# A gated feed-forward and a linear attention in one kernel: order written by hand against order left to the framework's scheduler

## The chip, the cores and the metric

The kernel runs on one core of one Trainium2 chip. The metric is the device time of one execution in microseconds; where several executions are shown, their median counts.

A core has five engines, each with its own instruction queue that is worked off in order: TensorE (PE in the profile, matrix products; PEld is its weight loads), VectorE (DVE), ScalarE (ACT), GpSimd (POOL) and SyncE (SP, which here only issues DMAs). They wait for one another on semaphores. An instruction that waits holds up everything behind it on its engine, whether that is ready or not. So for each engine the order of its instructions is part of the program, and it is this order that the two kernels differ in.

## The reference

Two branches read the same layer-normalised input of 2048 tokens by 512 channels; their sum and the input itself are the output.

```python
xn = layernorm(x)
return x + A(xn, wqkv, w_phi, wo) + B(xn, w_gate, w_up, w_down)

def A(x, wqkv, w_phi, wo):                    # 32 heads of 16 channels
    q, k, v = heads(x @ wqkv)
    pq, pk = q @ w_phi, k @ w_phi             # per head
    phi_q = concat(softmax(pq), softmax(-pq)) # likewise phi_k from pk
    kv = phi_k.T @ v                          # summed over all tokens
    z  = sum over tokens of phi_k
    o  = (phi_q @ kv) / (phi_q @ z + 1e-6)
    return o @ wo

def B(x, w_gate, w_up, w_down):               # 1792 hidden channels
    return ((x @ w_gate) * (x @ w_up)) @ w_down
```

Matrix data are bf16, sums are f32. Branch A needs `kv` over all tokens before any token's output can start; branch B (called the GLU below) needs only its own tokens.

## The kernel before

Tokens are handled in 16 tiles `n` of 128, and in 4 groups `T` of 512. All names and lines of this section are those of the kernel before.

**Inputs and head.** Every load is issued from SP, in the order written (lines 86 to 99): two single tiles of x, the small `w_phi`, the key part of `wqkv` transposed by the DMA (`wkT`), the value part `wv`, then x and the GLU weights in growing pieces. Ten matrix products on zeros (`warm`, L130) run while the first x is on its way. `LNs`, `LNr` and `LNx` normalise one tile: statistics on DVE (L198, L200), the reciprocal root by two ACT instructions (L204, L205), the scaling on DVE (L209). The channel-major copy `xnT` that the products need is made by PE for tiles 0 to 3 (`TRpe`), and for groups 1 to 3 by a store to DRAM and a transposing DMA back (`TRst`). `foldj` multiplies `w_phi` into the key weights (`W1k`) and later into the query weights (`W1q`), one 128-row block at a time.

**Key pass, one step per tile** (loop at L323). `PK` makes the products for the keys, `EX` takes both exponentials on ACT, `RED`, `RCP` and `PHI` (L273, L279, L284) sum, invert and scale them on DVE, `VV` makes the values, and `KV` adds eight small products into three PSUM banks that stay open over all tiles. In each step the program puts three GLU units `G` at chosen places. A unit is one 128-channel block `f` of the hidden layer for one token group: four products with `wg` (L143), a copy to SBUF on ACT (L146), four products with `wu` (L149) and the elementwise product on DVE (L151) into `hT`. The PSUM results come from one pool of three buffers (`ps_gu`, tag `gu`), shared with the output stage.

**Query pass, one step per tile** (loop at L414). The sums are masked into `KVZ` (L364, L367). `Pq` makes the query products and exponentials of a quarter group. `ND` makes numerators and denominators with eight small products into one four-bank PSUM tile (`nd`, one buffer), and a chain on DVE finishes them: `rsm` (L393), `rho` (L395), `tmp` (L397), `sm` (L400), `rden` (L402). The next `ND` may start when `sm` has read the tile. POOL makes the output tokens `o_tok` (L404), which go to DRAM and come back transposed, once per group, into the place of `xnT`. `Fin` makes a tile's output: 14 products with `wd` (L161) and 4 with `wo` (L164) into a `gu` buffer, the residual sum on DVE (L166), the store. From the sixth step on, each step runs one `Fin` beside one `ND`, and the last `Fin` is cut into two column halves.

**What sets the order.** `ctx.enter_context(tc.manual_schedule())` (L63) keeps every engine's instructions in the order in which the program writes them; the calls in the two loops are that order. Memory places and semaphores are still set by the framework.

Of the kernel before, what the change touches and what calls it, by code (L numbers as in the profile page):

```python
# [8 lines left out]
BF16 = mybir.dt.bfloat16  # L9
# [12 lines left out]
def kernel(  # L22
# [35 lines left out]
    wT_pool = ctx.enter_context(tc.tile_pool(name="wT", bufs=1))  # L58
    hpool = ctx.enter_context(tc.tile_pool(name="hpool", bufs=1))
    gpool = ctx.enter_context(tc.tile_pool(name="gpool", bufs=3))  # L60
    opool = ctx.enter_context(tc.tile_pool(name="opool", bufs=3))
    ps_gu = ctx.enter_context(tc.tile_pool(name="ps_gu", bufs=3, space=PSUM))
    ctx.enter_context(tc.manual_schedule())  # L63
# [8 lines left out]
    xnT = xpool.tile([P, DC, S], BF16, name="xnT")  # L72
    oT = xnT
    W1k = wpool.tile([P, DC, D], BF16, name="W1k")
    W1q = wpool.tile([P, DC, D], BF16, name="W1q")
    KVZ = wpool.tile([P, 2, CQ, HC, J], BF16, name="KVZ")
    hT = [hpool.tile([P, FC, TT], BF16, name=f"hT{T}") for T in range(NT // GT)]
# [4 lines left out]
    def dma_cols(w, src, slo, lo, hi, eng):  # L82
        eng.dma_start(out=w[:, :, lo:hi], in_=src[:, slo + lo:slo + hi].rearrange("(c p) f -> p c f", p=P))

    wkT = wT_pool.tile([P, DC, D], BF16, name="wT")
    dma_x(0, 1)
    dma_x(1, 2)
    nc.sync.dma_start(out=wphi[:], in_=A_w_phi.rearrange("(c h) d f -> (h d) c f", c=DC))
    nc.sync.dma_start_transpose(out=wkT[:], in_=A_wqkv[:, D:2 * D])  # L89
    dma_cols(wv, A_wqkv, 2 * D, 0, D, nc.sync)  # L90
    dma_x(2, 4)
    for lo, hi in ((0, 256), (256, 768)):
        dma_cols(wg, B_w_gate, 0, lo, hi, nc.sync)
        dma_cols(wu, B_w_up, 0, lo, hi, nc.sync)
    dma_x(4, 8)
    dma_cols(wg, B_w_gate, 0, 768, F, nc.sync)
    dma_cols(wu, B_w_up, 0, 768, F, nc.sync)
# [6 lines left out]
    warm = consts.tile([P, TT], BF16, name="warm")  # L104
    nc.vector.memset(warm[:], 0.0)
    ident = consts.tile([P, P], BF16, name="ident")
    make_identity(nc, ident[:])

    BO16 = consts.tile([P, HC, DH], BF16, name="BO16")
    nc.gpsimd.memset(BO16[:], 1.0)  # L110
    nc.gpsimd.affine_select(out=BO16[:], in_=BO16[:], pattern=[[-DH, HC], [0, DH]],
                            compare_op=ALU.is_ge, fill=0.0, base=0, channel_multiplier=1)
    nc.gpsimd.affine_select(out=BO16[:], in_=BO16[:], pattern=[[DH, HC], [0, DH]],
                            compare_op=ALU.is_ge, fill=0.0, base=DH - 1, channel_multiplier=-1)
    NVT = 4
# [3 lines left out]
    BD = wT_pool.tile([P, DC, HC, DH], BF16, name="BD")  # L119
    for c in range(DC):  # L120
        nc.gpsimd.tensor_tensor(out=BD[:, c], in0=BO16[:],
                                in1=_bcast_ap(wphi[:, c, :], [wphi.ap[0], [0, HC], [1, DH]]), op=ALU.mult)
# [5 lines left out]
    wps = ps_gu.tile([P, TT], F32, name="gu")  # L128
    for i in range(10):
        nc.tensor.matmul(wps[:], lhsT=warm[:, 0:P], rhs=warm[:], start=True, stop=True)  # L130

    glu_done = [0]

    def G(k=1):
        for _ in range(k):
            i = glu_done[0]
            if i >= FC * (NT // GT):
                return
            glu_done[0] += 1
            T, f = divmod(i, FC)  # L140
            gps = ps_gu.tile([P, TT], F32, name="gu")
            for c in range(DC):
                nc.tensor.matmul(gps[:], lhsT=wg[:, c, f * P:(f + 1) * P], rhs=xnT[:, c, T * TT:(T + 1) * TT],  # L143
                                 start=(c == 0), stop=(c == DC - 1))
            g_sb = gpool.tile([P, TT], BF16, name="g_sb")
            nc.scalar.copy(out=g_sb[:], in_=gps[:])  # L146
            ups = ps_gu.tile([P, TT], F32, name="gu")
            for c in range(DC):
                nc.tensor.matmul(ups[:], lhsT=wu[:, c, f * P:(f + 1) * P], rhs=xnT[:, c, T * TT:(T + 1) * TT],  # L149
                                 start=(c == 0), stop=(c == DC - 1))  # L150
            nc.vector.tensor_tensor(out=hT[T][:, f, :], in0=ups[:], in1=g_sb[:], op=ALU.mult)  # L151

    def Fin(n, parts=1):
        T, t4 = divmod(n, GT)
        o_sb = opool.tile([P, D], BF16, name="o_sb")
        w = D // parts
        for i in range(parts):
            sl = slice(i * w, (i + 1) * w)
            fin = ps_gu.tile([P, w], F32, name="gu")
            for f in range(FC):  # L160
                nc.tensor.matmul(fin[:], lhsT=hT[T][:, f, t4 * P:(t4 + 1) * P], rhs=wd[:, f, sl],  # L161
                                 start=(f == 0), stop=False)
            for c in range(DC):
                nc.tensor.matmul(fin[:], lhsT=oT[:, c, n * P:(n + 1) * P], rhs=wo[:, c, sl],  # L164
                                 start=False, stop=(c == DC - 1))
            nc.vector.tensor_tensor(out=o_sb[:, sl], in0=fin[:], in1=xall[:, n, sl], op=ALU.add)  # L166
            nc.sync.dma_start(out=out_view[:, n, sl], in_=o_sb[:, sl])

    a2e = ctx.enter_context(tc.tile_pool(name="a2e", bufs=2))
    Es = {}  # L170

    def Pq(T, cq, pool, tag):
        if cq == 0:
            Es[T] = a2e.tile([P, 2, CQ, TT], BF16, name="E")
        pq = pool.tile([P, TT], F32, name=tag)
        for j in range(DC):
            nc.tensor.matmul(pq[:], lhsT=W1q[:, j, cq * P:(cq + 1) * P], rhs=xnT[:, j, T * TT:(T + 1) * TT],  # L177
                             start=(j == 0), stop=(j == DC - 1))
        nc.scalar.activation(out=Es[T][:, 0, cq, :], in_=pq[:], func=AF.Exp, scale=1.0)  # L179
        nc.scalar.activation(out=Es[T][:, 1, cq, :], in_=pq[:], func=AF.Exp, scale=-1.0)  # L180

    with tc.tile_pool(name="ln", bufs=4) as lnpool, \
            tc.tile_pool(name="xn", bufs=2) as xnpool, \
            tc.tile_pool(name="a1s", bufs=2) as a1s, \
            tc.tile_pool(name="a1k", bufs=2) as a1k, \
# [3 lines left out]
        xns = {}  # L189

        mvs, rsts = {}, {}

        def LNs(n):
            ng, ni = divmod(n, GT)
            if ni == 0:
                xns[ng] = xnpool.tile([P, GT, D], BF16, name="xn")
            stats = lnpool.tile([P, nc.vector.BN_STATS_DIM], F32, name="stats")
            nc.vector.bn_stats(out=stats[:], in_=xall[:, n, :])  # L198
            mv = mvs[n] = lnpool.tile([P, nc.vector.BN_AGGR_DIM], F32, name="mv")
            nc.vector.bn_aggr(out=mv[:], in_=stats[:])  # L200

        def LNr(n):
            rstd = rsts[n] = lnpool.tile([P, 1], F32, name="rstd")
            nc.scalar.activation(out=rstd[:], in_=mvs[n][:, 1:2], func=AF.Ln, bias=eps_t[:], scale=1.0)  # L204
            nc.scalar.activation(out=rstd[:], in_=rstd[:], func=AF.Exp, scale=-0.5)  # L205

        def LNx(n):
            ng, ni = divmod(n, GT)
            nc.vector.tensor_scalar(out=xns[ng][:, ni, :], in0=xall[:, n, :], scalar1=mvs[n][:, 0:1],  # L209
                                    scalar2=rsts[n][:], op0=ALU.subtract, op1=ALU.mult)  # L210

        def TRpe(n, on_dve=False):
            ng, ni = divmod(n, GT)
            tp = ps_gu.tile([P, DC, P], BF16, name="gu")
            for c in range(DC):
                nc.tensor.transpose(out=tp[:, c, :], in_=xns[ng][:, ni, c * P:(c + 1) * P], identity=ident[:])
            if on_dve:
                nc.vector.tensor_copy(out=xnT[:, :, n * P:(n + 1) * P], in_=tp[:])
            else:
                nc.scalar.copy(out=xnT[:, :, n * P:(n + 1) * P], in_=tp[:])  # L220

        xds = {}

        def TRst(m):
            ng, ni = divmod(m, GT)
            if ni == 1:
                xds[ng] = dpool.tile([TT, D], BF16, name=f"xd{ng}")
            nc.sync.dma_start(out=xds[ng][(ni - 1) * P:(ni + 1) * P, :].rearrange("(n p) d -> p n d", p=P),
                              in_=xns[ng][:, ni - 1:ni + 1, :])
            if ni == GT - 1:  # L230
                nc.sync.dma_start_transpose(out=xnT[:, :, ng * TT:(ng + 1) * TT], in_=xds[ng][:])

        kvb = [ps_kv.tile([P, D], F32, name=f"kv{b}") for b in range(3)]
        kvps = [t[:, 0:3 * (P + 2)].rearrange("p (k c) -> p k c", k=3) for t in kvb]

# [11 lines left out]
        def PK(n, pk=None):  # L247
            if pk is None:
                pk = ps_a1.tile([P, D], F32, name="pk")
# [73 lines left out]
        for n in range(NT):  # L323
# [4 lines left out]
            if n >= GT:  # L328
                VV(n)
# [125 lines left out]
```

## Time and profile before

| | |
|---|---|
| median of 3 runs | 233.14 us (232.88 to 233.33) |
| the profiled execution | 233.14 us, of which the span from first to last instruction is 231.4 us |
| what lies around the span | 1.74 us |
| PE busy | 223.1 us, 1236 products in the trace |
| DVE busy | 152.1 us |
| ACT busy | 86.3 us |
| POOL busy | 22.4 us |
| moved by DMA | 19.38 MB |

The page of a profile gives for each engine the busy time and then, in 40 equal slices of the span, the busy share in tenths. A group line names a source line, an engine, an operation and its tiles, followed by the count, the busy time in us, the mean duration of one in ns, and the idle time of the engine before these instructions with what ended it. Products overlap on PE, so the time that each adds is read from the starts in the timeline rather than from the mean duration. The chain of work that ended last is followed back from the last instruction. A timeline line has start and duration in us, the engine, the line, and in brackets how long the engine idled before it.

### The profile page before, as it was taken

Reading aid. Unit: us, or ns where it says so; the run is one execution under the profiler, and the core shown is the slowest. Engines: PE = TensorE matmul, PEld = TensorE weight load, DVE = VectorE, ACT = ScalarE, POOL = GpSimd, SP = SyncE. Lnnn points to the kernel's source line nnn. Section 1 sums busy time; section 2 is a strip of 40 time slices with the busy share of each in tenths; the row PEclk is TensorE's granted clock in tenths of the full one; section 3 lists DMA queues with packets and bytes.
Section 4 is the critical chain, followed back from the end, with each engine's and each line's share of the span. In section 5 each row is a group of like instructions: output and inputs, shape, how many; then the busy total and the mean of one; then the engine's idle time right before and its main releaser. Section 6 shows DMA issues by size and latency. Waiting matters only on the chain.

```text
span 231.4 us, 3286 instructions
## 1 busy us (share of the span) xinstructions
PE 223.1 (96%) x1236; PEld 111.8 (48%) x1260; DVE 152.1 (66%) x261; ACT 86.3 (37%) x177; POOL 22.4 (10%) x42
## 2 busy tenths in 40 slices
PE   7699999999999999999999999999999999999995
PEld 2444454454454444454455544554454545544454
DVE  5659999779777796775567447995555556762121
ACT  3565453554554545354555365441211110000000
POOL 6300000000000000000000001331112221121000
PEclk9999999999999999999999999999999999999999
DMA  6999214100230981400000000126115115214201
GB/s 117 303 363 372 75 47 91 42 8 0 68 70 3 251 289 50 89 0 0 4 0 0 0 3 24 37 52 138 48 46 138 45 47 136 91 49 100 83 25 45
DMA packets 33825, 19.38 MB, mean 84 GB/s; under 512 B 20112, under 2 KB 32784, under 8 KB 33808
## 3 DMA queue, kind: packets, MB, share of 16 engines
q1 hardware_dynamic: 33808, 19.16, 29.3%
q8 instruction: 10, 0.16, 0.3%
q14 instruction: 7, 0.06, 0.1%
HBM read 8.67 MB, written 5.77 MB: 62 GB/s over the span
## 4 chain that ended last, share of the span: by engine, by line
PE 90%; DMA 4%; SPq 2%; DVE 1%; issue 1%; ACT 1%
PE gu L149 21%; PE gu L143 21%; PE gu L161 20%; PE gu L164 6%; PE pk L251 5%; PE vp L264 5%; PE pq L177 4%; PE nd L387 3%; DMA xall<-in_A_x_dram 2%; DMA xnT<-od_1573 2%; PE kv_182 L291 1%; PE kv_183 L291 1%; SPq L89 1%; PE kv_184 L291 1%; PE vp L177 1%
## 5 line engine op out<-in xcount | busy, mean ns | idle before, releaser
L149 PE MATMUL gu<-xnT,wu 128*128 128x512 bf16 x222 | 57.4, 379 | 0.2
L143 PE MATMUL gu<-xnT,wg 128*128 128x512 bf16 x218 | 56.8, 379 | 0.3
L146 ACT CAST g_sb<-gu 128x512 bf16<-128x512 f32 x56 | 32.9, 588 | 26.6 <-PE gu L143 25.6
L404 POOL TENSOR_TENSOR o_tok<-sm,rden 128x512 bf16<-128x512 f32 x16 | 16.9, 1057 | 184.5 <-DVE rden L402 181.2
L166 DVE TENSOR_TENSOR o_sb<-gu,xall 128x512 bf16<-128x512 f32 (+1 forms) x17 | 11.2, 661 | 35.7 <-PE gu L164 33.6
L149 PEld LDWEIGHTS <-wu 128*128 128x128 bf16 x224 | 21.9, 98 | 26.4
L143 PEld LDWEIGHTS <-wg 128*128 128x128 bf16 x224 | 21.3, 98 | 22.9
L179 ACT ACTIVATE E<-pq 128x512 bf16<-128x512 f32 x12 | 7.2, 597 | 34.9 <-PE pq L177 34.9
L273 DVE TENSOR_REDUCE sums<-e 128x64 f32<-128x1024 f32 x16 | 19.4, 1210 | 1.0 <-ACT e L259 0.9
L284 DVE TENSOR_TENSOR phik<-e,rs 128x1024 bf16<-128x1024 f32 x16 | 19.6, 1225 | 0.6
L164 PE MATMUL gu<-wo,xnT 128*128 128x512 bf16 (+1 forms) x65 | 16.3, 366 | 0.5 <-DMA xnT<-od_1573 0.4
L151 DVE TENSOR_TENSOR hT_97<-gu,g_sb 128x512 bf16<-128x512 f32 x14 | 9.7, 691 | 10.6 <-PE gu L149 10.6
L151 DVE TENSOR_TENSOR hT_96<-gu,g_sb 128x512 bf16<-128x512 f32 x14 | 9.6, 688 | 9.4 <-PE gu L149 9.4
L258 ACT ACTIVATE e<-pk 128x512 f32<-128x512 f32 x15 | 9.0, 597 | 17.1 <-PE pk L251 14.8
L264 PE MATMUL vp<-wv,xnT 128*128 128x512 bf16 x52 | 14.0, 379 | 1.0 <-DMA wv<-in_A_wqkv_dram 0.9
L251 PE MATMUL pk<-W1k,xnT 128*128 128x512 bf16 x58 | 15.0, 379 | 0.0
L161 PE MATMUL gu<-wd,hT_97 128*128 128x512 bf16 (+1 forms) x69 | 12.9, 336 | 0.1
L209 DVE TENSOR_SCALAR xn<-xall,mv,rstd 128x512 bf16<-128x512 bf16 x16 | 7.6, 483 | 8.0 <-ACT rstd L205 7.9
L198 DVE BATCH_NORM_STATS2 stats<-xall 128x6 f32<-128x512 bf16 x16 | 10.9, 679 | 2.9 <-DMA xall<-in_A_x_dram 2.9
L161 PE MATMUL gu<-wd,hT_96 128*128 128x512 bf16 x55 | 12.7, 379 | 0.1
L161 PE MATMUL gu<-wd,hT_95 128*128 128x512 bf16 x55 | 12.7, 379 | 0.1
L161 PE MATMUL gu<-wd,hT_94 128*128 128x512 bf16 x55 | 12.7, 379 | 0.1
(95 smaller groups left out, 248.8 us busy)
## 6 DMA issues: line engine op xcount, KB each, us to landing
out_dram<-o_sb SPq DMA_DIRECT2D x15, 128.0 KB, 1.7
wd<-in_B_w_down_dram SPq DMA_DIRECT2D x1, 1792.0 KB, 9.0
xall<-in_A_x_dram SPq DMA_DIRECT2D x3, 512.0 KB, 11.3
wg<-in_B_w_gate_dram SPq DMA_DIRECT2D x1, 1024.0 KB, 8.9
wu<-in_B_w_up_dram SPq DMA_DIRECT2D x1, 1024.0 KB, 10.8
wv<-in_A_wqkv_dram SPq DMA_DIRECT2D x1, 512.0 KB, 4.6
wg<-in_B_w_gate_dram SPq DMA_DIRECT2D x1, 512.0 KB, 6.3
wu<-in_B_w_up_dram SPq DMA_DIRECT2D x1, 512.0 KB, 7.3
```

The source lines that it names most:

```text
L143: nc.tensor.matmul(gps[:], lhsT=wg[:, c, f * P:(f + 1) * P], rhs=xnT[:, c, T * TT:(T + 1) * TT], start=(c == 0), stop=(c == DC - 1))
L146: nc.scalar.copy(out=g_sb[:], in_=gps[:])
L149: nc.tensor.matmul(ups[:], lhsT=wu[:, c, f * P:(f + 1) * P], rhs=xnT[:, c, T * TT:(T + 1) * TT], start=(c == 0), stop=(c == DC - 1))
L151: nc.vector.tensor_tensor(out=hT[T][:, f, :], in0=ups[:], in1=g_sb[:], op=ALU.mult)
L161: nc.tensor.matmul(fin[:], lhsT=hT[T][:, f, t4 * P:(t4 + 1) * P], rhs=wd[:, f, sl], start=(f == 0), stop=False)
L164: nc.tensor.matmul(fin[:], lhsT=oT[:, c, n * P:(n + 1) * P], rhs=wo[:, c, sl], start=False, stop=(c == DC - 1))
L177: nc.tensor.matmul(pq[:], lhsT=W1q[:, j, cq * P:(cq + 1) * P], rhs=xnT[:, j, T * TT:(T + 1) * TT], start=(j == 0), stop=(j == DC - 1))
L251: nc.tensor.matmul(pk[:], lhsT=xnT[:, j, n * P:(n + 1) * P], rhs=W1k[:, j, :], start=(j == 0), stop=(j == DC - 1))
L264: nc.tensor.matmul(vp[:], lhsT=xnT[:, j, n * P:(n + 1) * P], rhs=wv[:, j, :], start=(j == 0), stop=(j == DC - 1))
L273: nc.vector.tensor_reduce(out=sums[:], in_=ev, axis=AX.X, op=ALU.add)
L284: nc.vector.tensor_tensor(out=phik[:].rearrange("p s (h f) -> p (s h) f", f=DH), in0=ev, in1=rss[n][:].to_broadcast((P, 2 * H, DH)), op=AL ...
L404: nc.gpsimd.tensor_tensor(out=o_tok[:].rearrange("p (a h d) -> p a h d", a=2, d=DH), in0=sm[:, :, :, 0:DH], in1=rden[:].to_broadcast((P, 2 ...
```

## The change

The changed kernel computes the same with the same products, apart from the ten on zeros, which it leaves out. What differs:

- `manual_schedule` is gone. The framework's scheduler now decides for every engine in which order its instructions are issued; the program is written stage after stage: normalisation and folding, the key pass tile by tile, the query pass group by group, then the GLU and the outputs group by group. The scheduler may move later work ahead, product by product.
- The four loads `w_phi`, `wv` and the first 512 columns of `wg` and `wu` are issued from ACT's queue, ahead of ACT's table load. The rest stay on SP: x in pieces of 1, 3, 4, 4, 4 tiles, the GLU weights in pieces of 512 and 1280 columns.
- The transposes of group 0 go through the one-buffer tags `pk` and `vp`, which the folds (`pk`) and values (`vp`) use too; all folds are copied out by ACT.
- The normalised groups 1 to 3 go to DRAM in one store of four tiles each rather than two of two. That transposing DMAs are used for both weight parts, for groups 1 to 3 and for the attention output is as before; so is the pool of three PSUM buffers for the GLU.
- `oT` has memory of its own; the outputs have their own two PSUM buffers (`ps_fin`); the last output is not halved; three value tiles `vt` rather than four, three `phik` buffers rather than two, two `o_tok` buffers rather than three, two sets of normalisation scalars rather than four.

```diff
-    ctx.enter_context(tc.manual_schedule())
...
     dma_x(0, 1)
-    dma_x(1, 2)
-    nc.sync.dma_start(out=wphi[:], in_=A_w_phi.rearrange("(c h) d f -> (h d) c f", c=DC))
-    nc.sync.dma_start_transpose(out=wkT[:], in_=A_wqkv[:, D:2 * D])
-    dma_cols(wv, A_wqkv, 2 * D, 0, D, nc.sync)
-    dma_x(2, 4)
-    for lo, hi in ((0, 256), (256, 768)):
-        dma_cols(wg, B_w_gate, 0, lo, hi, nc.sync)
-        dma_cols(wu, B_w_up, 0, lo, hi, nc.sync)
+    dma_x(1, 4)
+    dma_wT(wkT, D)
+    nc.scalar.dma_start(out=wphi[:], in_=A_w_phi.rearrange("(c h) d f -> (h d) c f", c=DC))
+    dma_cols(wv, 0, A_wqkv, 2 * D, 3 * D, nc.scalar)
+    dma_cols(wg, 0, B_w_gate, 0, 512, nc.scalar)
+    dma_cols(wu, 0, B_w_up, 0, 512, nc.scalar)
     dma_x(4, 8)
-    dma_cols(wg, B_w_gate, 0, 768, F, nc.sync)
-    dma_cols(wu, B_w_up, 0, 768, F, nc.sync)
+    dma_cols(wg, 512, B_w_gate, 512, F)
+    dma_cols(wu, 512, B_w_up, 512, F)
     dma_x(8, 12)
     dma_x(12, 16)
...
-    wps = ps_gu.tile([P, TT], F32, name="gu")
-    for i in range(10):
-        nc.tensor.matmul(wps[:], lhsT=warm[:, 0:P], rhs=warm[:], start=True, stop=True)
...
+        def ln_group(ng):
+            mv = lnpool.tile([P, GT, nc.vector.BN_AGGR_DIM], F32, name="mv")
+            rstd = lnpool.tile([P, GT], F32, name="rstd")
+            xn = xnpool.tile([P, GT, D], BF16, name="xn")
+            for ni in range(GT):
+                n = ng * GT + ni
+                stats = lnpool.tile([P, nc.vector.BN_STATS_DIM], F32, name="stats")
+                nc.vector.bn_stats(out=stats[:], in_=xall[:, n, :])
+                nc.vector.bn_aggr(out=mv[:, ni, :], in_=stats[:])
+                nc.scalar.activation(out=rstd[:, ni:ni + 1], in_=mv[:, ni, 1:2], func=AF.Ln, bias=eps_t[:], scale=1.0)
+                nc.scalar.activation(out=rstd[:, ni:ni + 1], in_=rstd[:, ni:ni + 1], func=AF.Exp, scale=-0.5)
+                nc.vector.tensor_scalar(out=xn[:, ni, :], in0=xall[:, n, :], scalar1=mv[:, ni, 0:1],
+                                        scalar2=rstd[:, ni:ni + 1], op0=ALU.subtract, op1=ALU.mult)
+                if ng == 0:
+                    tp = ps_a1.tile([P, DC, P], BF16, name=("pk" if ni % 2 == 0 else "vp"))
+                    for c in range(DC):
+                        nc.tensor.transpose(out=tp[:, c, :], in_=xn[:, ni, c * P:(c + 1) * P], identity=ident[:])
+                    nc.scalar.copy(out=xnT[:, :, n * P:(n + 1) * P], in_=tp[:])
+            if ng > 0:
+                xd = dpool.tile([TT, D], BF16, name=f"xd{ng}")
+                nc.sync.dma_start(out=xd[:].rearrange("(n p) d -> p n d", p=P), in_=xn[:])
+                nc.sync.dma_start_transpose(out=xnT[:, :, ng * TT:(ng + 1) * TT], in_=xd[:])
...
+        def fold(wT, W1):
+            for j in range(DC):
+                wps = ps_a1.tile([P, D], F32, name="pk")
...
+                nc.scalar.copy(out=W1[:, j, :], in_=wps[:])
...
+        ln_group(0)
+        fold(wkT, W1k)
+        for n in range(NT):
+            if n % GT == 0 and n > 0:
+                ln_group(n // GT)
+            a1_tile(n)
...
+    with tc.tile_pool(name="opool", bufs=3) as opool, \
+            tc.tile_pool(name="ps_fin", bufs=2, space=PSUM) as ps_fin:
+        for T in range(S // TT):
+            hT = hpool.tile([P, FC, TT], BF16, name="hT")
+            for f in range(FC):
+                gps = ps_gu.tile([P, TT], F32, name="gu")
...
+                ups = ps_gu.tile([P, TT], F32, name="gu")
...
+                g_sb = gpool.tile([P, TT], BF16, name="g_sb")
+                with tc.high_priority():
+                    nc.scalar.copy(out=g_sb[:], in_=gps[:])
+                    nc.vector.tensor_tensor(out=hT[:, f, :], in0=ups[:], in1=g_sb[:], op=ALU.mult)
+            for t4 in range(GT):
+                n = T * GT + t4
+                fin = ps_fin.tile([P, D], F32, name="fin")
...
```

`a1_tile(n)` holds the products, exponentials, sums, scalings and `KV` of one tile in the forms of `PK`, `EX`, `VV`, `RED`, `RCP`, `PHI` and `KV`; the query pass holds the forms of `Pq` and `ND`.

## The prediction

> **What bounds the kernel now.** I read the page's busy times and slices first, then busy time by stage, then the chain that ended last, then the timeline of the head and of the query pass.
>
> ```profile
> PE 223.1 (96%) x1236; PEld 111.8 (48%) x1260; DVE 152.1 (66%) x261; ACT 86.3 (37%) x177; POOL 22.4 (10%) x42
> PE   7699999999999999999999999999999999999995
> DVE  5659999779777796775567447995555556762121
> PE 90%; DMA 4%; SPq 2%; DVE 1%; issue 1%; ACT 1%
> ```
>
> TensorE bounds it. DVE is two thirds busy, unevenly: 9 of 10 tenths in slices 4 to 7, then less.
>
> ```profile
> 13.60:40.60 27.00, 26.89 (x141) 13.03 (x143) 24.67 (x42) 13.26 (x31) 0.00 (x0) 1.00 0.55 177
> 40.60:129.00 88.40, 87.87 (x484) 43.59 (x492) 64.14 (x91) 44.56 (x90) 0.00 (x0) 1.00 0.21 57
> 129.00:155.40 26.40, 25.93 (x158) 13.36 (x160) 19.30 (x42) 13.59 (x26) 5.13 (x5) 1.00 0.07 21
> 155.40:228.60 73.20, 72.31 (x403) 37.09 (x409) 35.27 (x71) 7.60 (x14) 11.79 (x12) 1.00 0.30 79
> ```
>
> Each line: stretch, its length, then busy time of PE, PEld, DVE, ACT, POOL. From 13.6 to 228.6 us PE is busy 213.0 of 215.0: nothing is left to win there. What a new order can lose is read from DVE: 24.7 of 27.0 us in the first stretch, so early in the key pass DVE has little slack.
>
> ```profile
> 1.29 4.45 PE L130 MATMUL gu<-warm 128*128 128x512 bf16 x10 [1.29 <-DVE warm L105]
> 2.95 0.69 DVE L198 BATCH_NORM_STATS2 stats<-xall 128x6 f32<-128x512 bf16 x1 [1.72 <-DMA xall<-in_A_x_dram]
> 4.57 2.06 DVE L209 TENSOR_SCALAR xn<-xall,mv,rstd 128x512 bf16<-128x512 bf16 x2
> 10.03 0.69 DVE L198 BATCH_NORM_STATS2 stats<-xall 128x6 f32<-128x512 bf16 x1 [1.15 <-DMA xall<-in_A_x_dram]
> 10.99 1.03 PE L251 MATMUL kv_182<-W1k,xnT 128*128 128x512 bf16 x4
> ```
>
> The head: the first tile is normalised as soon as it has landed (2.95), and the first key product runs at 10.99. The DMA rate of the first 30 us, in 40 slices of 0.75 us:
>
> ```profile
> GB/s 0 0 94 251 44 135 169 288 200 254 324 376 327 282 334 358 354 351 350 350 366 393 388 374 391 388 382 377 352 362 339 149 23 52 307 0 0 0 0 0
> ```
>
> It is far from full before 7.5 us and then 282 to 393.
>
> ```profile
> L151 DVE TENSOR_TENSOR hT_94<-gu,g_sb 128x512 bf16<-128x512 f32 x14 | 9.5, 681 | 1.9 <-PE gu L149 1.9
> L284 DVE TENSOR_TENSOR phik<-e,rs 128x1024 bf16<-128x1024 f32 x16 | 19.6, 1225 | 0.6
> L273 DVE TENSOR_REDUCE sums<-e 128x64 f32<-128x1024 f32 x16 | 19.4, 1210 | 1.0 <-ACT e L259 0.9
> 147.84 0.68 PE L387 MATMUL nd<-KVZ,E 128*128 128x144 bf16 x8
> 148.71 0.35 DVE L393 RECIPROCAL rsm<-nd 128x32 f32<-128x32 f32 x1
> 150.15 0.72 DVE L400 TENSOR_TENSOR sm<-nd,tmp 128x544 f32<-128x544 f32 x1
> 150.94 0.66 PE L387 MATMUL nd<-KVZ,E 128*128 128x144 bf16 x8
> ```
>
> The first three give DVE's prices. The last four give the shortest cycle of the one `nd` buffer: 150.94 - 147.84 = 3.1 us.
>
> **The change, part by part.** Transposing DMAs and the three `gu` buffers exist already; what changes is order. I take it from the built program, engine by engine. Prices on PE, start to start in the timeline: four products of 512 columns 0.86, so 0.216 each; a fold's four 0.23; the eight of `KV` 0.47; the eight of `ND` 0.50. All of it: 928 x 0.216 + 8 x 0.23 + 16 x 0.47 + 16 x 0.50 = 217.8 us, as before without the warm-up. So the sum is: when PE gets going, what it waits, the tail.
>
> *Head.* In the new DVE order the statistics of tile 4, which wait for the load of tiles 4 to 7, stand before the four normalisations of group 0. So everything waits for that load. On SP it follows x0, x1-3 and `wkT`: 1.57 MB with itself; ACT's queue moves 1.57 MB beside it. With the gaps filled from about 2.2 us, 3.1 MB at 340 GB/s land at 11.4. If ACT's loads took nothing from it, it would land as the before's 1.55 MB did, at 10.0; if the transpose slows it, 13. I take 11.4, nearest to the plateau rate. The Trainium skill, "DMA: Bandwidth & Descriptors", section Issuing engines are not separate DMA queues, says that DMAs from several engines share the same 16 engines and save only issue time. The trace has one queue and cannot show it; by that rule the load lands at 11.4, by separate queues at 10.0, and the sum falls by 1.4.
>
> Statistics 0.69 and four scalings of 0.41: 13.7. Transposes go through two one-buffer tiles, copied by ACT at 0.58 each: first fold at 15.3. The folds share one buffer, so each waits for ACT's copy of the last (0.6), and ACT has five root instructions (1.2 us) and two value copies (1.2) in between: fold copies end at 16.9, 18.7, 19.9 and 21.7, and the first key product starts at 21.8. Values and five GLU products run meanwhile, so PE loses less than this delay.
>
> The warm-up goes. Its ten products took 0.445 each, later ones 0.216: early work runs at half speed while the granted clock reads 1.00. Lost at most what it took from the ten, 2.2 us; nothing, if ACT's copies set the pace. I take 0.5, near the low end, because they do: 22.3. The skill, "TensorE: Matmul & The Clock Gate", Part 1, says that the first 3.4 us or so of activity after idling run at half clock; by that page an estimate is 1.7 us instead of 0.5, and the sum rises by 1.2. Issuing four loads before the table load costs ACT 2.0 us (0.43 + 0.57 + 0.47 + 0.51); the table is then there at 4.1 and hidden, as nothing is scaled before 11.4; without that cover 0.2 over 3.90.
>
> *First half of the key pass (eight tiles, GLU group 0).* The first `RED` starts after `PK` 0.86, a `g_sb` copy and the exponentials (1.1), at 24.7. From there to the last product of group 0, DVE's order has 8 x (1.21 + 0.58 + 1.22) = 24.1, 13 GLU products at 0.685 = 8.9, six statistics and eight aggregations 5.0, eight scalings 3.2, and 0.3 for the second `EX`: 41.5, to 66.2. PE has 36.5 in the same stretch. DVE bounds, because the scheduler brings normalisation of group 3 forward and gives a tile 1.75 GLU units where the old order gave three. The next tile also needs group 2: its last scaling ends 34.7 into the stretch (59.4), the store 2.6 to 3 (rows of 256 KB: 2.1 to 2.6), the transpose 4.3: 66.9. The two meet; 66.9.
>
> *Second half (tiles 8 to 15).* Little GLU work is left beside it: PE has 28.9 us. DVE: first `PK` and `EX` 2.3, eight tiles 24.1, five products 3.4, `KVZ` 1.7 (132.46 to 134.15), 31.5; and 1.2, since twice `RED` waits for an exponential whose `PK` waited for the one buffer. 32.7, to 99.6. Between 30 (more beside each other) and 36 (0.5 per tile).
>
> *Query pass.* `ND`s stand 11 to 16 products apart (2.4 to 3.5 us plus 0.50). The cycle on DVE is 3.1 us with no product inside, 3.8 with one. PE has 245 x 0.216 + 8.0 = 60.9; waits of 0.1 to 0.3 for most of the sixteen, 2.5. Without waits 60.9; with one more product in each cycle 72. Most gaps are 14 products, 3.5 us, so near the low end: 63.4, to 163.0.
>
> *Outputs and GLU group 3.* Twelve outputs en bloc, 105 GLU products, four outputs: 393 x 0.216 = 84.8. DVE needs 0.69 per 3.9 us or per 1.73 us, so it costs nothing; if the GLU's three buffers failed to hide product and copy, 0.1 for each of 13 units. `oT` has long landed. To 247.8.
>
> *Tail.* 2.8 us from PE's end (228.56) to the span's end; the whole last output adds 0.69 - 0.42 on DVE and 1.7 - 1.5 landing: 3.3. Span 251.1; 1.74 lies around it as in the profiled execution, whose 233.14 is the median too: **252.8 us**.
>
> At nothing: the new stores to DRAM of four tiles (group 1 lands near 28, wanted after 30; cover gone, it delays one for one), SP's weight loads `wd` and `wo` (wanted at 163), the fewer `vt` and `o_tok` buffers (POOL busy 10%; if `o_tok` waited on its store, 1.7 us at one tile).
>
> **The rivals.**
>
> *PE stays the bound.* The scheduler's fill hides DVE: waits of the key and query pass vanish. For it: PE's 36.5 against DVE's 41.5 is close, and old DVE rows hold latency. Against it: DVE's sum is made of busy times alone. Time: first fold 15.3 + 217.8 + about 2 lost in the folds + 3.3 + 1.7 = 240.
>
> *The token chain is the bound.* Each `ND` waits for one product more and `rden`, 0.69 + 0.35, so 16 x 1.04 = 16.6 in place of 2.5. For it: DVE's order puts one or two GLU products inside almost every chain. Against it: those have mostly been ready since before the chain. Time: 267.
>
> *Not slower.* One mechanism, in the head: the tiles 4 to 7 arrive early, since a second queue fills the idle DMA time before 7 us, and PE starts at 7 instead of 15.3; with PE then the bound, 240 - 8.3 = 231.7. It decides only if that load lands before 4.5 us (1.57 MB in 2.5 us, 630 GB/s); the highest rate in the trace is 393.
>
> **How the numbers follow.** Forecast 0.76, PE the bound 0.10, token chain 0.12, not slower 0.02. Uncertain terms: landing -1.4 to +1.6, cold clock -0.5 to +1.7, first half -3 (DVE's waits beside PE's) to +3, second half -2.7 to +3.3, query pass -2.5 to +8.6, GLU +1.3. Their ends do not fall together; the range goes from 244, between forecast and first rival, to 263, towards the second. A measurement tells 0.2% (0.5 us) from no change. Faster 0.02, same 0.01, slower 0.97.
>
> **What would show it.** The first `xn` should end near 12.5 and the first key product start near 22, with DVE waiting for the x load before; DVE should be busy over nine tenths until 66 with PE losing some 7 us there; tiles 8 to 15 should take about 33 us; the outputs should start near 163 and run without gaps. I am wrong if PE's busy share stays at 96%, if tiles 4 to 7 land well off 11.4, or if gaps lie in the last 85 us.

## The result and the profile after

The changed kernel takes 251.29 us (median of 4, 250.54 to 252.31) against 233.01 for the kernel before on the same chip: a ratio of 1.079, 95% interval 1.074 to 1.083. It is slower, and the forecast of 252.8 was 1.5 us too high. Its profiled execution took 251.78 us with a span of 250.1, 18.7 more than before.

The page of the changed kernel, busy times, two rows of slices and the chain by engine:

```profile
PE 224.5 (90%) x1208; PEld 108.4 (43%) x1232; DVE 145.3 (58%) x255; ACT 88.0 (35%) x181; POOL 22.1 (9%) x41
...
PE   0009999999899999999999999999999999999993
...
DVE  4126599999589995587788998712112124344121
...
PE 65%; DVE 19%; DMA 7%; SPq 2%; ACT 2%; issue 2%; DVEq 0%; ACTq 0%
```

PE's busy time has hardly changed; its share fell from 96% to 90% because three slices at the start are empty. DVE is now 19% of the chain that ended last.

The same kernel's windows: stretch, length, busy time of PE, PEld, DVE, ACT, POOL. The bounds are the first key product, that of tile 8, the first `ND`, the first output and PE's end:

```profile
26.74:67.42 40.68, 39.42 (x224) 19.45 (x227) 37.00 (x60) 22.26 (x52) 0.00 (x0) 1.00 0.44 118
67.42:97.97 30.55, 30.04 (x189) 14.94 (x193) 27.15 (x35) 18.79 (x35) 0.00 (x0) 1.00 0.11 27
97.97:161.30 63.33, 62.67 (x367) 31.05 (x374) 50.08 (x103) 29.89 (x54) 15.84 (x15) 1.00 0.24 57
161.30:246.20 84.90, 84.48 (x386) 38.39 (x393) 20.29 (x30) 7.62 (x13) 1.06 (x1) 1.00 0.11 32
```

Priced by the starts of products (0.216 us each, as in the prediction), PE's work in these four stretches is 39.0, 28.9, 60.9 and 84.9. So PE waits 1.7, 1.7, 2.4 and 0.0 us: 5.8, against 1.4 over the same work before.

At 26.74 the changed kernel has as many 512-column products still to run (913) as the kernel before at 13.6. So of the 18.7 us **13.1 are lost ahead of that point**, 4.4 in the waits behind it, and 1.1 in the tail (PE's end to the span's end 3.9, before 2.8). The timeline of the changed kernel shows the head, and further down three DVE starts that are used below:

```profile
1.74 5.01 SPq L75 DMA_TRANSPOSE wT<-in_A_wqkv_dram  x1
...
6.80 0.57 SPq L68 DMA_DIRECT2D xall<-in_A_x_dram  x1
...
17.33 0.69 DVE L140 BATCH_NORM_STATS2 stats<-xall 128x6 f32<-128x512 bf16 x1 [10.36 <-DMA xall<-in_A_x_dram]
17.94 1.36 DVE L144 TENSOR_SCALAR xn<-xall,mv,rstd 128x512 bf16<-128x512 bf16 x4
...
21.03 0.59 PE L165 MATMUL pk<-BD,wT 128*128 128x128 bf16 x4 [0.28 <-ACT rstd L143]
...
26.74 1.02 PE L174 MATMUL pk<-W1k,xnT 128*128 128x512 bf16 x3
...
38.89 1.21 DVE L191 TENSOR_TENSOR phik<-e,rs 128x1024 bf16<-128x1024 f32 x1
40.02 0.69 DVE L286 TENSOR_TENSOR hT<-gu,g_sb 128x512 bf16<-128x512 f32 x1
40.62 0.55 DVE L189 RECIPROCAL rs<-sums 128x64 f32<-128x64 f32 x1
```

As predicted, the statistics of tile 4 stand ahead of the four scalings and wait for tiles 4 to 7 (10.36 us). But that load lands at 17.3, not at 11.4: SP issues it at 6.80 only, since issuing the transposing load of `wkT` ahead of it took 5.01 us (2.38 before). And that load itself is slow, by the same trace's DMA issues (last number: us from issue to landing; before 4.8):

```profile
wT<-in_A_wqkv_dram SPq DMA_TRANSPOSE x1, 13.8
```

Beside it, ACT's queue loads `wv` and the first columns of `wg` and `wu`, 1.5 MB. **Theory 1**: these loads slow the transposing DMA, and DVE's order then lets everything wait. **Rivals**: DVE's order alone, or the folds' one buffer with ACT's copies, or a slow `wkT` for reasons of its own.

### The profile page after: what moved, and what is told of

Its sections match the earlier page's. It is cut to its first block, busy times and chain, and to the rows that moved or that the text cites. A ratio compares the mean times of both kernels' runs of the same rounds, so it can differ in the third digit from the quotient of the medians.

```text
span 250.1 us, 3214 instructions
## 1 busy us (share of the span) xinstructions
PE 224.5 (90%) x1208; PEld 108.4 (43%) x1232; DVE 145.3 (58%) x255; ACT 88.0 (35%) x181; POOL 22.1 (9%) x41
## 4 chain that ended last, share of the span: by engine, by line
PE 65%; DVE 19%; DMA 7%; SPq 2%; ACT 2%; issue 2%; DVEq 0%; ACTq 0%
PE fin L291 19%; PE gu L280 13%; PE gu L275 12%; PE fin L294 5%; PE pq L234 5%; DVE sums L187 5%; DVE phik L191 4%; DMA xall<-in_A_x_dram 4%; DVE hT L286 3%; PE nd L245 3%; PE vp L181 2%; PE pk L174 2%; SPq L75 2%; DVE rs L189 2%; DMA xnT<-xd_512 2%
## 5 line engine op out<-in xcount | busy, mean ns | idle before, releaser
L286 DVE TENSOR_TENSOR hT<-gu,g_sb 128x512 bf16<-128x512 f32 x56 | 38.4, 686 | 23.6 <-PE gu L280 19.6
L291 PE MATMUL fin<-wd,hT 128*128 128x512 bf16 x220 | 50.6, 379 | 0.2
L297 DVE TENSOR_TENSOR o_sb<-fin,xall 128x512 bf16<-128x512 f32 x16 | 11.1, 692 | 51.6 <-PE fin L294 48.5
L291 PEld LDWEIGHTS <-hT 128*128 128x128 bf16 x224 | 21.8, 98 | 26.7 <-DVE sm L258 0.5
L149 PE MATMUL pk<-ident,xn 128*128 128x128 bf16 x8 | 1.2, 303 | 18.6 <-DVE xn L144 18.4
L181 PE MATMUL vp<-wv,xnT 128*128 128x512 bf16 x62 | 17.7, 394 | 0.1
L234 PE MATMUL pq<-xnT,W1q 128*128 128x512 bf16 x62 | 16.8, 378 | 0.1
L294 PE MATMUL fin<-wo,oT 128*128 128x512 bf16 x62 | 16.2, 379 | 0.1
L237 ACT ACTIVATE E<-pq 128x512 bf16<-128x512 f32 x16 | 9.6, 597 | 13.7 <-PE pq L234 11.9
L258 DVE TENSOR_TENSOR sm<-nd,tmp 128x544 f32<-128x544 f32 x16 | 11.5, 720 | 0.7
L255 DVE TENSOR_TENSOR tmp<-nd,rho 128x544 f32<-128x544 f32 x16 | 11.6, 723 | 0.4
## 6 DMA issues: line engine op xcount, KB each, us to landing
wg<-in_B_w_gate_dram ACTq DMA_DIRECT2D x1, 512.0 KB, 12.4
```

Source lines behind the costliest of these rows:

```text
L181: nc.tensor.matmul(vp[:], lhsT=xnT[:, j, n * P:(n + 1) * P], rhs=wv[:, j, :], start=(j == 0), stop=(j == DC - 1))
L286: nc.vector.tensor_tensor(out=hT[:, f, :], in0=ups[:], in1=g_sb[:], op=ALU.mult)
L291: nc.tensor.matmul(fin[:], lhsT=hT[:, f, t4 * P:(t4 + 1) * P], rhs=wd[:, f, :], start=(f == 0), stop=False)
```

## The experiments

Most runs use the changed kernel's program with its instructions frozen in the scheduler's order, so that single ones can be moved (`order` is the list of their places). Readings from the profiled execution of each, in us:

| kernel | `wkT` takes | first fold | first key product | from there to the span's end | median time |
|---|---|---|---|---|---|
| changed | 13.8 | 21.03 | 26.74 | 223.4 | 251.29 |
| e1 frozen | 9.5 | 16.31 | 21.96 | 223.2 | 250.12 |
| e2 norms first | 12.4 | 17.67 | 24.27 | 223.2 | 249.06 |
| e3 loads on SP | 4.8 | 12.55 | 19.26 | 224.3 | 245.40 |
| e4 both | 5.0 | 10.93 | 18.12 | 225.6 | 246.06 |
| e5 head cleared | 5.2 | 10.30 | 16.52 | 229.4 | 247.57 |
| e6 and warm-up | 5.3 | 9.98 | 17.37 | 227.3 | 246.49 |
| e9 and `wqT` behind | 5.0 | 9.86 | 18.24 | 226.9 | 247.71 |
| e10 less on DVE | 13.1 | 20.39 | 26.09 | 220.9 | 248.74 |
| e12 plain `wkT` | 6.7 | 15.16 | 20.77 | 223.1 | 246.22 |

**e1, the frozen order.**

> The changed kernel's instructions, written out by hand in the order that its scheduler chose, so that single instructions can be moved in what follows. Nothing else differs but the place of one memset on POOL. Every theory: the changed kernel's time, 251.3 us within 0.5, first key product at 26.7.

250.12 (246.88 to 251.11), with one execution far below the 251.3 within 0.5 that was expected. The profiled execution is that one, 246.88, with a first key product 4.8 us earlier and the rest unchanged. It differs from the changed kernel's in how long `wkT` took, 9.5 against 13.8, with the same loads beside it; the four times of this one program spread over 4.2 us. Later runs are therefore read from the first key product on where the head is not the question.

**e2, the normalisations first.**

```diff
+    order.remove(183)  # bn_stats of tile 4: behind the four normalisations of group 0
+    order.insert(order.index(184), 183)
```

> One instruction of the frozen order is moved: the statistics of tile 4 go behind the four normalisations of group 0 on DVE. Theory 1 (two causes in series: DVE's order makes PE wait for tiles 4 to 7, landed at 17.3, and behind that stands the transposing load of wkT, landed near 15.5): normalisations and transposes are done by about 8 us, the first fold waits for wkT and starts near 15.8 in place of 21.0, first key product near 21.5, time near 246. Theory 2 (DVE's order alone is the head's loss): first fold near 9, time near 239. Theory 3 (the head is limited by ACT's copies and the one fold buffer, the wait is beside that): less than 1 us, 250.5 to 251.

249.06 (248.66 to 250.37), 1 us less than e1 and within its spread. The transposes ran at 8.35 as theory 1 has it, and `wkT` had landed by 14.1; yet the first fold waited on, by the timeline:

```profile
17.67 0.58 PE L215 MATMUL pk<-BD,wT 128*128 128x128 bf16 x4 [6.97 <-ACT rstd L219]
```

What released it is ACT's `rstd` of tile 4: in ACT's order too, tile 4's `rstd` instructions stand ahead of or between the copies of tiles 2 and 3 that the fold's buffer waits for. Theory 2, the order of DVE alone, is refuted: it asked for 239. Theory 1 missed that the same wait stands on a second engine. Theory 3, the folds' one buffer with ACT's copies, is not settled by this run.

**e3, the loads on SP.**

```diff
-    dma_cols(wv, 0, A_wqkv, 2 * D, 3 * D, nc.scalar)
-    dma_cols(wg, 0, B_w_gate, 0, 512, nc.scalar)
-    dma_cols(wu, 0, B_w_up, 0, 512, nc.scalar)
...
+    dma_cols(wv, 0, A_wqkv, 2 * D, 3 * D)
+    dma_cols(wg, 0, B_w_gate, 0, 512)
+    dma_cols(wu, 0, B_w_up, 0, 512)
...
+    for k in (4, 5, 6):  # wv and the first columns of wg and wu: on SP, behind tiles 4 to 7
+        order.remove(k)
+    i7 = order.index(7) + 1
+    order[i7:i7] = [4, 5, 6]
```

> The frozen order with the loads of wv and the first 512 columns of wg and wu moved from ACT's queue to SP's, behind tiles 4 to 7; DVE's order as in the changed kernel. Theory 1 (loads on a second queue slow the transposing DMA): wkT takes about 5 us again, SP issues tiles 4 to 7 near 3, they land near 9, the first fold starts near 12.7, the first key product near 18.5, time near 243. Rival (the transposing DMA takes 13.8 us for a reason of its own, such as the three x tiles ahead of it in one load): its landing and that of tiles 4 to 7 stay, wv, wg and wu come after 17 us, time 251 to 254.

245.40 (245.30 to 246.50), 4.7 less than e1, and the scatter is 1.2 us in place of 4.2. The DMA issues of this run:

```profile
xall<-in_A_x_dram SPq DMA_DIRECT2D x1, 512.0 KB, 4.3
...
wT<-in_A_wqkv_dram SPq DMA_TRANSPOSE x1, 4.8
```

`wkT` takes 4.8 again and tiles 4 to 7 land at 8.8: these loads beside it were the cause, and the rival falls. The edit changes their queue and their place behind tiles 4 to 7 together, so it does not tell which of the two counts. The first key product came 0.8 later than expected, and a new wait took 1.1 us:

```profile
21.62 1.29 DVE L231 BATCH_NORM_STATS2 stats<-xall 128x6 f32<-128x512 bf16 x2 [6.53 <-DMA xall<-in_A_x_dram]
...
27.47 0.64 PE L215 MATMUL kv<-vt,phik 128*128 128x129 bf16 x8 [1.07 <-DVE phik L282]
```

DVE's order has the statistics of tiles 8 and 9 ahead of the first `RED`, and tiles 8 to 11 are loaded behind the rest of `wg` and `wu`.

**e4, both moves.**

> Both moves together. Theory 1: first fold when wkT has landed, near 7.5, fold chain 5.7 to 7, first key product near 14, at which PE then waits a little for wv and the GLU weights; time near 238.5, of which 4.4 over the kernel before is the steady part. If ACT's copies and the one fold buffer were the limit: first key product not before 18, time 243 or more.

246.06 (245.27 to 246.75), no better than e3. The first key product came at 18.12 and not at 14, which is what was expected if ACT's copies and the one fold buffer set the pace. The fold waited again for tile 4's `rstd` on ACT, and from there to the key product it took 7.2 us, with slow products among them:

```profile
10.93 0.58 PE L215 MATMUL pk<-BD,wT 128*128 128x128 bf16 x4 [1.09 <-ACT rstd L219]
```

What was gained, 1.1 us, was lost at the first `phik`, where PE now waited 2.3.

**e5, what stood next in line.** On top of e4:

```diff
+    i6 = order.index(6) + 1  # tiles 8 to 11 ahead of the other columns of wg and wu
+    order.remove(10)
+    order.insert(i6, 10)
+    for k in (185, 186, 190):  # Ln and Exp of tile 4, Ln of tile 5 on ACT: behind the copies of tiles 2 and 3 and of the first fold
+        order.remove(k)
+    i79 = order.index(79) + 1
+    order[i79:i79] = [185, 186, 190]
+    order.remove(187)  # the scaling of tile 4 needs them
+    order.insert(order.index(186) + 1, 187)
```

> The kernel of the run with both moves, with two more things taken out of the way that its trace shows next in line: on ACT the Ln and Exp of tile 4 and the Ln of tile 5 go behind the copies of tiles 2 and 3 and of the first fold (there the first fold waited 1.1 us for them), and on SP tiles 8 to 11 go ahead of the other columns of wg and wu (there DVE stood 8.2 us before the statistics of tile 8, and PE lost 2.3 us at the first phik). Theory 1, as amended (a stack of waits for loads that the chosen order puts ahead of ready work, each hiding the next): first fold near 10, first key product near 17, no wait of over 1 us at the first phik, span less first key product 223.3 as in the changed kernel, time near 242. Rival (the head is at its floor, the folds' one buffer and the slow clock set it): first key product at 18 again, time 244 to 245.

247.57 (246.52 to 248.16): slower than e4, against both theories. The head did get shorter (16.52), and the waits for tile 4 and at `phik` went; but the timeline has the first product of tile 4's values, and the windows after it (PE busy first, granted clock third from the end):

```profile
29.92 1.46 PE L215 MATMUL vp<-wv,xnT 128*128 128x512 bf16 x3 [4.39 <-DMA xnT<-xd]
```

```profile
27.00:30.00 3.00, 0.08 (x1) 0.09 (x2) 2.88 (x4) 0.00 (x0) 0.00 (x0) 0.57 0.87 188
30.00:33.00 3.00, 2.78 (x13) 1.62 (x15) 0.00 (x0) 0.29 (x1) 0.00 (x0) 0.50 0.99 330
33.00:36.00 3.00, 3.00 (x13) 1.22 (x12) 0.07 (x1) 0.90 (x2) 0.00 (x0) 0.79 1.07 362
```

PE waits 4.4 us for `xnT` of group 1, and after the gap the clock is granted at 0.50 to 0.79 for six microseconds.

**e6, the warm-up as well.** Ten products on zeros ahead of e5's first.

> The same with the ten warm-up products of the kernel before put back ahead of everything on PE. If the slow clock sets the fold chain (four folds' columns in 0.59 us, against 0.39 later): chain from first fold to first key product 5.7 in place of 7, first key product near 15.5, time near 240.5. If ACT's copies set it: within 0.3 us of the run without.

246.49 (246.13 to 246.74), 1.1 us less than e5, which neither expectation had; PE's wait for `xnT` of group 1 is 3.40 us in place of 4.39. The first key product is no earlier (17.37). PE idled 2.02 us between the warm-up and the first transposes, and the warm-up's effect was gone by 9 us, as this window of the run shows (clock 0.50):

```profile
9.00:12.00 3.00, 2.45 (x14) 1.15 (x12) 2.55 (x7) 2.61 (x8) 0.00 (x0) 0.50 1.07 366
```

**e7, the other way round.** The kernel before, its order untouched, with the changed kernel's loads in its head.

```diff
-    dma_x(1, 2)
-    nc.sync.dma_start(out=wphi[:], ...)
+    nc.scalar.dma_start(out=wphi[:], ...)
+    dma_x(1, 4)
     nc.sync.dma_start_transpose(out=wkT[:], in_=A_wqkv[:, D:2 * D])
-    dma_cols(wv, A_wqkv, 2 * D, 0, D, nc.sync)
...
+    dma_cols(wv, A_wqkv, 2 * D, 0, D, nc.scalar)
+    dma_cols(wg, B_w_gate, 0, 0, 512, nc.scalar)
+    dma_cols(wu, B_w_up, 0, 0, 512, nc.scalar)
```

> The kernel before, its order untouched, with only its head's loads issued as in the changed kernel: wphi, wv and the first 512 columns of wg and wu on ACT's queue, x tiles 1 to 3 in one load. Theory 1 (loads on a second queue slow the transposing DMA): wkT takes 9.5 to 14 us in place of 4.8, the first fold starts 4 to 8 us later than 7.1, time 237 to 241. Rival (a second queue only fills idle DMA time): 232 to 233.5.

241.08 (240.20 to 242.60) against 233.34: 7.7 us, ratio 1.034 (1.030 to 1.038). `wkT` took 12.8 us, and the first fold stood at 14.56 in place of 7.09:

```profile
14.56 1.04 PE L236 MATMUL kv<-BD,wT 128*128 128x128 bf16 x8 [7.14 <-DMA wT<-in_A_wqkv_dram]
```

So the changed kernel's loads alone cost the hand-written order 7.7 us, with no scheduler in it.

**e8, the kernel before without its warm-up.**

> The kernel before without its ten warm-up products. By the bounds of the prediction 0 to 2.2 us more, its own figure 0.5; if the slow clock lasts through the first folds and values as in the trace of the changed kernel (three products in 1.44 us, later 0.65), near 235.

233.94 (233.29 to 234.36, 10 executions), ratio 1.0020 (1.0002 to 1.0037): 0.6 us, barely clear of noise. In the profiled execution (234.22) the first key product comes 1.66 us later than at 10.99, and most of that is not in the median time:

```profile
12.65 1.24 PE L248 MATMUL kv<-W1k,xnT 128*128 128x512 bf16 x4
```

**e9, `wqT` behind group 1.** On top of e6:

```diff
+    order.remove(513)  # transposing load of wqT on SP: behind that of xnT, group 1
+    order.insert(order.index(204) + 1, 513)
```

> The run with the cleared head and the warm-up, with one load moved on SP: the transposing load of wqT, whose issue held SP for 8.1 us there, goes behind that of xnT for group 1, for which PE then waited 3.4 us. Theory 1 (every wait removed so far uncovered the next one, and this is the one that is late now): the wait goes, first key product stays near 17, span less first key product near 223.3 as in the changed kernel, granted clock near 1, time near 242. Rival (DMA as a whole is what is late: 3.4 us of transfers are still to come, whoever is first): xnT lands late all the same, time 245 to 246.5.

247.71 (246.77 to 248.57): the rival was nearer, though its 245 to 246.5 was still too low. PE still waits for `xnT` of group 1, though its transposing load no longer stands behind that of `wqT`:

```profile
30.04 1.11 PE L215 MATMUL vp<-wv,xnT 128*128 128x512 bf16 x2 [2.79 <-DMA xnT<-xd]
```

The store of `xd`, issued at 14.51, took 10.7 us behind the weight loads (10.9 in e5, 5.2 in the changed kernel).

**e10, less work on DVE.**

```diff
-        E(lambda: nc.vector.tensor_reduce(out=sums()[:], in_=ev(), axis=AX.X, op=ALU.add))
+        E(lambda: nc.vector.tensor_reduce(out=sums()[:], in_=ev()[:, :, 0:DH // 2], axis=AX.X, op=ALU.add))
...
-            rho = lazy("a2s", [P, 2, 2 * HC, 1], F32, "rho")
-            E(lambda: nc.vector.tensor_tensor(out=rho()[:], in0=ndv(0)[:, :, :, DH + 1:DH + 2], in1=rsm()[:],
-                                              op=ALU.mult))
+            rho = rsm
+            E(lambda: None)
```

> The frozen order with less work on DVE, at the price of the result: each RED sums 8 of its 16 features (about 0.6 us less for each of 16 tiles), and rho is left out of each ND's chain, tmp taking rsm in its place (0.2 to 0.35 us less for each of 16). Read from the first key product on, since the head varies from run to run. If DVE sets the waits of PE there: the first half of the key pass goes from 40.7 to 39.2 (PE alone 39.0), the second from 30.6 to 29.2 (28.9), the query pass from 63.3 to 61.5 (60.9), span less first key product from 223.3 to 219.5. If PE's waits there are for its own buffers and not for DVE: 223 again.

Its windows, at the same bounds as those of the changed kernel:

```profile
26.09:65.94 39.85, 38.97 (x223) 19.43 (x226) 33.29 (x60) 22.47 (x52) 0.00 (x0) 1.00 0.44 120
65.94:95.54 29.60, 29.25 (x190) 15.44 (x194) 23.43 (x35) 18.70 (x35) 0.00 (x0) 1.00 0.12 29
95.54:158.29 62.75, 62.28 (x366) 31.22 (x374) 47.25 (x87) 29.89 (x54) 15.86 (x15) 1.00 0.24 57
```

0.8, 1.0 and 0.6 us less, 2.5 in all to the span's end, where 3.8 were expected if DVE set every wait. So DVE sets at least about half of PE's waits in the key pass (1.8 of 3.4); most of its work there is still in this run, so the other half may be its too. In the query pass 0.6 of 2.4 went; what the rest waits for stays open.

**e11, the kernel before with `wkT` first.** SP starts with the transposing load; x tile 0, `wphi` and x tile 1 come over ACT's queue.

> The kernel before with the transposing load of wkT as SP's first instruction, and x tile 0, wphi and x tile 1, small loads, on ACT's queue. If what the runs have shown holds (PE starts when wkT has landed, and what slows wkT is large loads beside it): wkT lands near 5.7 in place of 7.0, wv near 8 in place of 9.2, first key product near 9.8 in place of 11.0, time 232.1 against 233.3. If any transfer on a second queue beside it slows it: 235 or more.

235.06 (233.13 to 236.69, 12 executions), ratio 1.0057 (1.0027 to 1.0088): 1.75 us more and not 1.2 less. The time is the one expected if any transfer on a second queue slows `wkT`, but it was not `wkT` that suffered. `wkT` was there by about 6.1 (5.3 us, as in e6 with nothing large beside it); now the small loads are late, `wphi` after 4.7 us in place of 2.0, x tile 1 at 6.51 in place of 3.78:

```profile
6.51 0.69 DVE L198 BATCH_NORM_STATS2 stats<-xall 128x6 f32<-128x512 bf16 x1 [2.47 <-DMA xall<-in_A_x_dram]
```

PE idled 3.1 us behind the warm-up, its products were slow until 13, and the first key product came at 14.1. So small loads on a second queue, 272 KB in all, were slow beside the transposing load, and the head lost more by them than it won.

**e12, a plain load of `wkT`.** The frozen order, everything else alike.

```diff
-    dma_wT(wkT, D)
+    E(lambda: nc.sync.dma_start(out=wkT()[:], in_=A_wqkv[:, D:2 * D].rearrange("(c p) f -> p c f", p=P)))
```

> The frozen order with wkT loaded by a plain DMA of the same 512 KB in place of the transposing one; what it leaves out is the transposition, so the folds get the wrong matrix. The loads of wv, wg and wu stay on ACT's queue beside it. If it is the transposing DMA that suffers from loads on a second queue: SP issues it in 0.6 us and tiles 4 to 7 right behind, wkT lands near 7, tiles 4 to 7 near 10, first fold near 13.7, first key product near 19.5, time near 243.5. If any load on SP would share the engines' time with ACT's 1.5 MB in the same way: wkT lands at 9.5 to 14 and tiles 4 to 7 at 13 to 17 as before, time 247 to 251.

246.22 (245.59 to 246.79), 3.9 less than e1. The DMA issues and the timeline:

```profile
wT<-in_A_wqkv_dram SPq DMA_DIRECT2D x1, 512.0 KB, 6.7
```

```profile
11.47 0.69 DVE L231 BATCH_NORM_STATS2 stats<-xall 128x6 f32<-128x512 bf16 x1 [4.19 <-DMA xall<-in_A_x_dram]
```

The same bytes beside the same loads on ACT's queue take 6.7 us plainly and 9.5 to 13.8 transposed, and SP issues them in 0.48 us in place of 4.3 to 5.0. The time does not fall to the expected 243.5; tiles 4 to 7 land at 11.5 and not near 10. The Trainium skill, "Advanced Engine Details and Errata", section X-Bar Transpose (TRN2), says that transposing DMAs on trn2 are as fast as regular ones. With no large load on the other queue the runs agree (4.7 to 5.3 us for 512 KB, and `wv` plainly 4.6); with 1.5 MB beside it they do not, and the measurement decides.

## Why the prediction was right, and where it was not

The time was right because two errors cancelled. Against the changed kernel's milestones, in us:

| step | predicted | measured | error |
|---|---|---|---|
| to the first key product | 22.3 | 26.74 | +4.4 |
| first half of the key pass | 44.6 | 40.68 | -3.9 |
| second half | 32.7 | 30.55 | -2.1 |
| query pass | 63.4 | 63.33 | -0.1 |
| outputs | 84.8 | 84.9 | +0.1 |
| tail | 3.3 | 3.9 | +0.6 |

*Head: right mechanism, one term mis-sized.* That everything waits for tiles 4 to 7 is what the trace shows. The term that failed is the landing at 11.4: bytes over the plateau rate, with 13 as the bound "if the transpose slows it". It was 17.3, because the transposing load beside ACT's loads took 13.8 us and held SP's next issue until 6.80. By its own sign, "if tiles 4 to 7 land well off 11.4", the prediction was wrong here, and the first `xn` ended near 18.4 and not near 12.5. Where the load of `wkT` is plain, tiles 4 to 7 land at 11.47, so the sharing rule that the prediction weighed (the Trainium skill, "DMA: Bandwidth & Descriptors", section Issuing engines are not separate DMA queues) gave the right number for plain loads; it makes no exception for a transposing one. From the landing to the first key product 10.9 us were predicted and 9.4 measured.

*First half: the sum of DVE durations.* "DVE bounds" was half right (e10): DVE was busy nine tenths of the stretch, but PE lost 1.7 us there and not some 7. The 41.5 us reckoned from the first `RED` to the last product of group 0 were 37.5 (29.55 to 67.1), since an instruction on DVE starts before the one ahead of it ends: in the timeline above `phik` lasts 1.21 and the next starts 1.13 later, the product 0.69 and 0.60. With such steps (`RED` and `PHI` 1.13, `RCP` 0.46, product 0.60, scaling 0.32) the same list adds up to 37.4. The timeline of before had these starts too. The other branch, the wait for group 2 at tile 8, ended the stretch (PE waited 0.68 us for it). Its time, 66.9 predicted and 67.42 measured, agrees by the same luck: the stretch began later than predicted, and the last scaling of group 2 ended 30.5 us behind the first `RED` (at 60.04) and not 34.7. The prediction's own terms for it add up to 66.3 to 66.7, not 66.9.

*Second half.* Same error, 24.1 for eight tiles; measured at the low end of the bounds given (30).

*Query pass, outputs, warm-up.* The 2.5 us of waits were 2.4 and the outputs ran without gaps. The 0.5 for the warm-up was 0.6 in the median time of the kernel before (e8); no run puts the warm-up into the changed kernel alone. The estimate of 1.7 worked out from the Trainium skill, "TensorE: Matmul & The Clock Gate", Part 1, which stood beside the sum, is what the first key product lost there (1.66), but too much for the time.

*Tail.* The whole last output and its longer store cost 1.1, not 0.5.

*The rivals.* "PE stays the bound" (240) and "the token chain is the bound" (267) fell: PE's waits behind the first key product are 5.8 us, and the query pass is 63.33. "Not slower" rested on a second queue that fills idle DMA time; e7 shows the opposite, 7.7 us lost by the loads issued this way.

*What the 18.7 us are.* Of the 13.1 in the head, the loads on ACT's queue are the part that is shown. Without them the first key product came 7.5 us earlier (26.74 to 19.26 between the two profiled executions), and the median fell by 4.7 against e1 and by 5.9 against the changed kernel. Another 5.7 of the head (19.26 in e3 against 13.6) was not won by any move tried: e4 to e9 brought the first key product forward by up to 2.7 us more, and none of them ran faster than e3. Two causes are left for it, and no run tested either by itself. One is how soon the order asks for tile 4, by these lines of the kernel before and of the changed one:

```profile
39.59 1.03 PE L251 MATMUL pk<-W1k,xnT 128*128 128x512 bf16 x4
...
35.59 0.81 PE L181 MATMUL vp<-wv,xnT 128*128 128x512 bf16 x3
```

The hand-written order asks for it 28.6 us after the first key product (10.99 to 39.59), filling the time with GLU units, the scheduler's order after 8.9 (26.74 to 35.59). So tiles 4 to 7 must be loaded, normalised, stored and brought back while the weights are still coming. The other is the chain of the folds: from the first fold to the first key product it took 5.6 to 8.4 us in every run of the changed order, and 3.9 in the kernel before (7.09 to 10.99), whose folds go through four tiles and not one buffer. But the kernel before without its warm-up takes 5.7 too (6.93 to 12.65 in e8), so slow early products have a part in it; how much is the buffer's stays open. Behind the head, DVE's relief is worth 2.5, and the tail 1.1; what the rest of the waits is for stays open.

## What to carry to other kernels

Price the first loads by kind and neighbours and not by bytes alone: here a transposing load took 4.8 us with every large load on its own queue and behind it, and up to 13.8 beside plain loads from a second one, and the waits behind it inherited the difference. Before clearing a wait at the head, find the next instruction on each engine that is ordered ahead of ready work; here each such wait that was cleared uncovered another, on DVE, on ACT and in the DMAs. For an engine's stretch add up starts, not durations.

## What was not expected of the hardware

- A transposing load of 512 KB beside 1.5 MB of plain loads on another queue took 9.5, 12.4, 12.8, 13.1 and 13.8 us in five executions, against 4.7 to 5.3 without them and 6.7 for a plain load beside them; its issue held SP for up to 5.0 us. Behind plain loads on its own queue such a load was slow too: in e3 to e6 the transposing load of `wqT`, issued behind the last weight loads, took 8.5, 9.4, 12.6 and 11.6 us, and its issue up to 9.04, as in this line of e5. Why, the runs do not show.

```profile
15.61 9.04 SPq L180 DMA_TRANSPOSE wT<-in_A_wqkv_dram  x1
```

- After a gap of 4.39 us on PE the clock was granted at 0.50 to 0.79 for six microseconds (e5), and after one of only 2.02 us, with 1.0 us of work in the 3.4 from the gap's start to 9 us, at 0.50 (e6). After 2.79 us it was 0.57 for three microseconds (e9); after 2.30 us in e4 it stayed at 1.00. The Trainium skill, "TensorE: Matmul & The Clock Gate", section Why this matters for your kernels, asks for no gap of over about 3 us; e5 agrees, and e6 and e9 show that here shorter ones could be enough.
